# Rebuilding the prologue of a fused Fourier-mixing and gated-FFN kernel

## The chip, the cores and the metric

The kernel runs on one core of a Trainium2 chip. The time is device time in microseconds (us), the median of several executions; lower is better. A core has five engines that work side by side: TensorE (PE in the profile) multiplies matrices, VectorE (DVE) and ScalarE (ACT) work on elements, GpSimd (POOL) does what is left, and SyncE (SP) only issues transfers. They meet at semaphores. Matrix products land in PSUM and the other operands lie in SBUF.

A ratio is the mean time of one kernel's runs over the mean of the other kernel's runs of the same rounds, so it is not quite the ratio of the medians that stand beside it. The profile's span is about 1.8 us shorter than the device time of the same execution.

## The reference

```python
X = np.fft.fft(x, axis=1)                    # x: 8 x 3008 x 256, float32
X = np.fft.fft(X, axis=2)
h = X.real.astype(np.float32).reshape(8 * 3008, 256)
gate = np.maximum(h @ w_gate, 0.0)           # w_gate, w_val: 256 x 1536
val = h @ w_val
out = (gate * val) @ w_out                   # w_out: 1536 x 256
```

The kernel never forms the Fourier transform along the last axis. It folds that transform into the two weight matrices, which it does once, and it exploits symmetry: a real input gives mirrored outputs, so half of the rows are enough for both products.

## The kernel before

Each of the eight batches passes through stage 1 (an add and subtract "fold" of x, then products with a cosine and sine matrix), a shuffle through DRAM, and stage 2. Then come 36 steps of 128 hidden columns: a gate product G, a value product V, their activation gs and product h, and the mirrored pair. The output product po of a step runs 12 steps later. Batch b+1 is prepared inside the steps of batch b. In the steps, GpSimd forms some mirrored products h and, between them, folds the x of a batch two ahead (`fold(b + 2, ...)`). For this text the important part is what runs before the first step, and the weight folds that spill into the first steps.

```python
FIRST = (0, 24, 8, 16)
def fold_first(r):                    # batch 0, 8 rows of 32 at a time, all on VectorE
    ...
    part(lo, 8, 1, ALU.add, False)
    ...                               # subtracts of the same rows
    nc.vector.tensor_copy(...)        # two columns of each row that have no partner

def fold_w(n, i, cs):                 # a weight tile of 512 columns times a 256-row cosine matrix
    ps = pso.tile([128, 512], F32, tag="o", name="psw")
    for c in range(2):                # two fp32 products that accumulate
        nc.tensor.matmul(ps[:], lhsT=cd[c][:, cs, :], rhs=wst[i, n, c][:], start=(c == 0), stop=(c == 1))
    ...                               # copies to wc, ws and (scaled) wm
...
for r in FIRST:
    fold_first(r)
for c0, c1 in ((1, 4), (4, 6), (6, 8), (0, 1)):
    for c in range(c0, c1):
        stage1(0, c, "act")
    shuffle_out(0, c0, c1)
for blk in range(NBLK):
    shuffle_in(0, 4 * blk, 4 * blk + 4)
load_w(1)
load_w(2)
...
nc.gpsimd.tensor_copy(si[0:1, 0:1], wst[1, 2, 1][0:1, 0:1])   # waits for the last weight
load_x(1, nc.sync)                    # a plain load, and a gather that GpSimd issues
for _ in fold(1, nc.gpsimd):
    pass
for i in range(2):
    for cs in range(2):
        fold_w(0, i, cs)              # 4 folds before the first step
rotate(0)
stage2(0, 0, 0, "act")
stage2(0, 0, 1, "dve")
...
for k in range(4):
    at(k, fold_w, 1, k // 2, k % 2)       # 8 folds inside steps 0 to 7
    at(4 + k, fold_w, 2, k // 2, k % 2)
    at(8 + k, stage2, 0, 1 + k // 2, k % 2, "dve")
```

Of the kernel before, what the change touches and what calls it, by code (L numbers as in the profile page):

```python
# [18 lines left out]
RND = 12582912.0  # L19

# [22 lines left out]
def kernel(ctx: ExitStack, tc, x, w_gate, w_val, w_out, out):  # L43
# [67 lines left out]
    FIRST = (0, 24, 8, 16)  # L111

    def load_first():
        xl = xp.tile([96, J, D], F32, tag="xl", name="xl")
        xh = xp.tile([96, NB // 2, D], F32, tag="xh", name="xh")
        for r in FIRST:
            nc.sync.dma_start(out=(xl if r < 16 else xh)[:, r % 16:r % 16 + 8, :],
                              in_=view(x, r * D, [[NB * D, 96], [1, 8 * D]]))
        xt[0] = [xl, xh] + [tp.tile([NA, J, D], BF16, tag="eo", name="eo") for i in range(2)]

    def fold_first(r):
        t, e = xt[0][r // 16][0:NA], xt[0][2 + r // 16]
        lo = r % 16

        def part(a, n, o, op, swap):
            p0 = free(t, a * D + 1, [D, n], [1, H - 1])
            p1 = free(t, a * D + D - 1, [D, n], [-1, H - 1])
            nc.vector.tensor_tensor(e[:, a:a + n, o:o + H - 1], p1 if swap else p0, p0 if swap else p1, op=op)

        part(lo, 8, 1, ALU.add, False)  # L130
        if r == 16:
            part(0, 1, H + 1, ALU.subtract, False)
            part(1, 7, H + 1, ALU.subtract, True)
        else:
            part(lo, 8, H + 1, ALU.subtract, r > 16)
        nc.vector.tensor_copy(free(e[:], lo * D, [D, 8], [H, 2]), free(t, lo * D, [D, 8], [H, 2]))
# [9 lines left out]
    def stage1(b, c, evac):  # L146
# [19 lines left out]
        dst = t1[:, 2 * c:2 * c + 2, :]  # L166
        src = ps[0:96, :].rearrange("p (i d) -> p i d", i=2)
# [47 lines left out]
    nc.gpsimd.iota(ix[:], pattern=[[2 * NA, B]], base=2 * NA - 1, channel_multiplier=-2)  # L215
    nc.gpsimd.tensor_scalar(ix[:], ix[:], scalar1=0, scalar2=None, op0=ALU.max)
    load_first()

# [11 lines left out]
    qpi = const.tile([128, 1], F32, tag="qpi")  # L230


    wst = {}
    for n in range(DF // 512):
        for i in range(2):
            for c in range(2):
                wst[i, n, c] = hp.tile([128, 512], F32, tag="h", name="wst")
    cd = [hp.tile([128, 2, H], F32, tag="h", name="cd") for c in range(2)]

    def load_w(n):  # L240
        for i, w in enumerate((w_gate, w_val)):
# [3 lines left out]
    def fold_w(n, i, cs):  # L245

        ps = pso.tile([128, 512], F32, tag="o", name="psw")
        for c in range(2):
            nc.tensor.matmul(ps[:], lhsT=cd[c][:, cs, :], rhs=wst[i, n, c][:], start=(c == 0), stop=(c == 1))  # L249
        sl_ = slice(n * 512, (n + 1) * 512)  # L250
        if cs == 0:
            nc.scalar.copy(wc[i][:, sl_], ps[:])
        else:
            (nc.scalar.copy if n == 0 else nc.vector.tensor_copy)(ws[i][:, sl_], ps[:])  # L254
            nc.scalar.activation(wm[i][:, sl_], ps[:], ACTF.Copy, scale=s2[:])
# [9 lines left out]
    load_w(0)  # L265

    with tc.tile_pool(name="sp", bufs=1, space=SB) as sp:
        def residue(t, q, n):

            nc.vector.tensor_scalar(q, t, scalar1=1.0 / n, scalar2=RND, op0=ALU.mult, op1=ALU.add)  # L270
            nc.vector.tensor_scalar(q, q, scalar1=-RND, scalar2=float(n), op0=ALU.add, op1=ALU.mult)
            nc.vector.tensor_tensor(t, t, q, op=ALU.subtract)
# [4 lines left out]
        def cosines(out, a, n):  # L277

            nc.scalar.activation(out, a, ACTF.Sin, scale=-2.0 * math.pi / n, bias=qpi[0:a.shape[0], :])


        w1h = sp.tile([NA, 16, 96], BF16, tag="w1h")
        si = sp.tile([NA, NB], F32, tag="si")
        nc.gpsimd.iota(si[:], pattern=[[1, NB]], base=0, channel_multiplier=NB,
                       allow_small_or_imprecise_dtypes=True)
        ki = sp.tile([NA, NKA, 4], F32, tag="ki")
        nc.gpsimd.iota(ki[:], pattern=[[1, NKA], [NKA, 4]], base=0, channel_multiplier=0,
                       allow_small_or_imprecise_dtypes=True)
        nc.vector.memset(qpi[:], math.pi / 2)
        tt = sp.tile([NA, NB, 48], F32, tag="tt")  # L290
        tq = sp.tile([NA, NB, 48], F32, tag="tq")
        nc.vector.tensor_tensor(tt[:], si[:].unsqueeze(2).to_broadcast([NA, NB, 48]),
                                free(ki[:], 0, [0, NB], [1, 48]), op=ALU.mult)
        residue(tt[:], tq[:], S)
        nc.scalar.activation(tq[:], tt[:], ACTF.Abs)
        nc.gpsimd.memset(wz[:], 0.0)
        nc.gpsimd.memset(w1[:, 0, :], 0.0)
# [6 lines left out]

        for r in FIRST:
            fold_first(r)
        for c0, c1 in ((1, 4), (4, 6), (6, 8), (0, 1)):
            for c in range(c0, c1):
                stage1(0, c, "act")
            shuffle_out(0, c0, c1)  # L310
        for blk in range(NBLK):
            shuffle_in(0, 4 * blk, 4 * blk + 4)
        load_w(1)
        load_w(2)


        mi = sp.tile([128, 2], F32, tag="mi")
        nc.gpsimd.iota(mi[:], pattern=[[128, 2]], base=0, channel_multiplier=1,
                       allow_small_or_imprecise_dtypes=True)
        dd = sp.tile([128, 2, H + 1], F32, tag="dd")  # L320
        nc.gpsimd.iota(dd[:], pattern=[[0, 2], [1, H + 1]], base=0, channel_multiplier=0,
                       allow_small_or_imprecise_dtypes=True)
        dq = sp.tile([128, 2, H + 1], F32, tag="dq")
        nc.vector.tensor_tensor(dd[:], dd[:], mi[:].unsqueeze(2).to_broadcast([128, 2, H + 1]), op=ALU.mult)
        residue(dd[:], dq[:], D)
        nc.scalar.activation(dq[:], dd[:], ACTF.Abs)
        for c in range(2):
            cosines(cd[c][:, 0, :], dq[:, c, 0:H], D)
            sines(cd[c][:, 1, 1:H], dd[:, c, 1:H], D, 1.0)
            cosines(cd[c][:, 1, 0:1], dq[:, c, H:H + 1], D)  # L330

        pl = nc.gpsimd


        pi = sp.tile([128, 1], I32, tag="pi")
        nc.gpsimd.iota(pi[:], pattern=[[0, 1]], base=0, channel_multiplier=1)

        def bits(shift, mask):
            ti = sp.tile([128, 1], I32, tag=f"b{shift}{mask}i")
            nc.vector.tensor_scalar(ti[:], pi[:], scalar1=shift, scalar2=mask,  # L340
                                    op0=ALU.logical_shift_right, op1=ALU.bitwise_and)
            tf = sp.tile([128, 1], F32, tag=f"b{shift}{mask}f")
            nc.vector.tensor_copy(tf[:], ti[:])
# [3 lines left out]
        z = sp.tile([128, 1], F32, tag="z")  # L347
        pl.tensor_scalar(z[:], jj[:], scalar1=0.0, scalar2=None, op0=ALU.is_equal)
        zs = sp.tile([128, 1], F32, tag="zs")
        pl.tensor_tensor(zs[:], z[:], sl[:], op=ALU.mult)  # L350
        mul = sp.tile([128, 1], F32, tag="mul")
        pl.tensor_scalar(mul[:], zs[:], scalar1=16.0, scalar2=None, op0=ALU.mult)
        pl.tensor_tensor(mul[:], mul[:], jj[:], op=ALU.add)
        offs = []

        for cs, (o0, d1) in enumerate(((8.0, -8.0), (16.0, -8.0))):
            o = sp.tile([128, 1], F32, tag=f"off{cs}")
            pl.tensor_scalar(o[:], sl[:], scalar1=d1, scalar2=o0 - 8.0, op0=ALU.mult, op1=ALU.add)
            nz = sp.tile([128, 1], F32, tag=f"nz{cs}")
            pl.tensor_scalar(nz[:], z[:], scalar1=-1.0, scalar2=1.0, op0=ALU.mult, op1=ALU.add)  # L360
            pl.tensor_tensor(o[:], o[:], nz[:], op=ALU.mult)
            pl.tensor_scalar(o[:], o[:], scalar1=8.0, scalar2=None, op0=ALU.add)
            offs.append(o)
        kbi = sp.tile([128, 4, NB], F32, tag="kbi")
        nc.gpsimd.iota(kbi[:], pattern=[[0, 4], [1, NB]], base=0, channel_multiplier=0,
                       allow_small_or_imprecise_dtypes=True)
        ui = sp.tile([128, 4, NB], F32, tag="ui")
        nc.gpsimd.iota(ui[:], pattern=[[1, 4], [0, NB]], base=0, channel_multiplier=0,
                       allow_small_or_imprecise_dtypes=True)
        nc.vector.tensor_scalar(ui[:], ui[:], scalar1=up[:], scalar2=None, op0=ALU.is_equal)  # L370
        for cs in range(2):
            t2 = sp.tile([128, 4, NB], F32, tag=f"m2t{cs}")
            nc.vector.tensor_scalar(t2[:], kbi[:], scalar1=mul[:], scalar2=offs[cs][:],
                                    op0=ALU.mult, op1=ALU.add)
            sv = sp.tile([128, 4, NB], F32, tag=f"m2s{cs}")
            sin_of(nc, nc.vector, sp, sv[:], t2[:], NB, [128, 4, NB])
            nc.vector.tensor_tensor(m2[:, cs, :].rearrange("p (u k) -> p u k", u=4), sv[:], ui[:], op=ALU.mult)


        di = sp.tile([128, 4, 2, 16], F32, tag="di")  # L380
        nc.gpsimd.iota(di[:], pattern=[[-32, 4], [-16, 2], [-1, 16]], base=0, channel_multiplier=1,
                       allow_small_or_imprecise_dtypes=True)
        ro = sp.tile([128, 4, 2, 16], F32, tag="ro")
        pl.memset(ro[:], 0.0)
        nc.vector.tensor_scalar(ro[:, :, 0, 1:16], di[:, :, 0, 1:16], scalar1=16.0, scalar2=-1.0,
                                op0=ALU.is_equal, op1=ALU.mult)
# [224 lines left out]
```

## Time and profile before

| what | before |
|---|---|
| device time | 670.34 us median of the first 3 runs (668.94 to 670.45) |
| span of the profiled execution | 667.6 us |
| TensorE busy | 631.9 us (95%) |
| first gate product G starts | 35.23 us |
| first output product po starts | 69.55 us |
| from there to the end | 598.03 us |

These lines are from the profile page: the busy time of each engine (with its share of the span and its number of instructions), and the chain of work that ended last, by engine.

```profile
PE 631.9 (95%) x4157; PEld 413.5 (62%) x4234; DVE 544.4 (82%) x863; ACT 429.2 (64%) x811; POOL 444.9 (67%) x618
...
PE 78%; POOL 9%; issue 5%; DVE 4%; DMA 2%; ACT 1%; SPq 0%; POOLq 0%; DVEq 0%
```

TensorE is the bound engine and only the first 70 us hold much idle time.

Next, the timeline. Columns are start, duration, engine, line of the kernel, operation, output and input with their shapes, and how many records the row joins; the bracket gives the engine's idle time just before and what ended it.

```profile
36.09 1.88 PE L249 MATMUL psw<-wst,cd 128*128 128x512 f32 x4
...
38.14 0.17 POOL L397 COPY si<-wst 1x1 f32<-1x1 f32 x1 [13.18 <-DMA wst<-in_moe_w_val_dram]
38.35 0.60 ACT L437 ACTIVATE gs<-G 128x512 f32<-128x512 f32 x1 [3.17 <-POOL si L397]
...
39.00 0.36 PE L447 MATMUL G<-pq,wm 128*128 128x480 bf16 x1 [1.02 <-ACT gs L437]
...
43.34 1.88 PE L249 MATMUL psw<-wst,cd 128*128 128x512 f32 x4
...
45.05 0.37 PE L447 MATMUL G<-pq,wm 128*128 128x480 bf16 x1
```

A weight fold is four fp32 passes. The next product starts 1.71 us after it (45.05 - 43.34; 1.72 us after others), so eight of them cost about 13.7 us of TensorE inside the steps. The first gs waits 3.17 us for a GpSimd copy that itself waits for the last weight.

At 60.91 ScalarE makes the scaled copy wm of a fold, for which it has waited on VectorE's plain copy ws; gs comes behind it, and TensorE waits for gs:

```profile
60.91 0.69 ACT L255 ACTIVATE wm<-psw,s 128x512 bf16<-128x512 f32 x1 [2.11 <-DVE ws L254]
...
61.94 0.60 ACT L437 ACTIVATE gs<-G 128x512 f32<-128x512 f32 x1
...
62.59 0.36 PE L447 MATMUL G<-pq,wm 128*128 128x480 bf16 x1 [0.96 <-ACT gs L437]
```

The third view is that of one line: the copies of the two unpaired columns on VectorE, with the shortest, median and longest duration in ns. GpSimd is idle at that time.

```profile
L136 DVE CAST eo<-xl x2: 196/198/200, 9.4 to 15.2; 94x16 bf16<-94x16 f32 x2
L136 DVE CAST eo<-xh x2: 199/200/202, 12.0 to 18.3; 94x16 bf16<-94x16 f32 x2
```

### The profile page before, as it was taken

How to read it: one execution, taken by the hardware profiler on the slowest of the kernel's cores; microseconds unless marked ns; L12 is line 12 of the kernel's file. 1: busy time of each engine (PE TensorE's matmuls, PEld its weight loads, DVE VectorE, ACT ScalarE, POOL GpSimd, SP SyncE). 2: the span in 40 equal slices, each digit the busy share in tenths (PEclk: the TensorE clock that was granted, in tenths of full speed). 3: DMA queues.
4: the chain of work that ended last, by engine and by line, in shares of the span. 5: the costliest groups of instructions: out<-in, count | busy, mean ns of one | idle time of the engine just before them, and what ended most of it. 6: DMA issues, size and time to landing. Idle time of an engine off the chain costs nothing.

```text
span 667.6 us, 12589 instructions
## 1 busy us (share of the span) xinstructions
PE 631.9 (95%) x4157; PEld 413.5 (62%) x4234; DVE 544.4 (82%) x863; ACT 429.2 (64%) x811; POOL 444.9 (67%) x618
## 2 busy tenths in 40 slices
PE   1889999999999999999999999999999999999996
PEld 1444666666566666666666666666666766666665
DVE  8446689889788887988888897888889798899991
ACT  5445676676666766676676766676666766666662
POOL 1218559977995599756996499756996455455451
PEclk9999999999999999999999999999999999999999
DMA  9693473185114922177112931258211241211213
GB/s 230 202 239 50 113 182 104 49 204 187 38 56 106 221 89 66 44 163 217 38 44 66 225 128 39 80 132 200 80 48 42 62 127 40 80 31 39 55 32 93
DMA packets 31845, 70.76 MB, mean 106 GB/s; under 512 B 4410, under 2 KB 21426, under 8 KB 29394
## 3 DMA queue, kind: packets, MB, share of 16 engines
q1 hardware_dynamic: 29444, 58.16, 32.0%
q0 software_dynamic: 2336, 11.80, 8.7%
q8 instruction: 33, 0.54, 0.4%
q14 instruction: 32, 0.26, 0.1%
HBM read 39.77 MB, written 30.96 MB: 106 GB/s over the span
## 4 chain that ended last, share of the span: by engine, by line
PE 78%; POOL 9%; issue 5%; DVE 4%; DMA 2%; ACT 1%; SPq 0%; POOLq 0%; DVEq 0%
PE po L503 33%; PE V L459 9%; PE G L436 9%; PE G L447 8%; PE V L457 7%; PE G L435 7%; POOL h L473 4%; POOL eo L101 3%; DMA xh<-in_x_dram 2%; POOL xl L98 2%; PE psw L249 2%; PE V L485 2%; PE ps L159 2%; DVE E L467 1%; PE ps L201 1%
## 5 line engine op out<-in xcount | busy, mean ns | idle before, releaser
L473 POOL TENSOR_TENSOR h<-gm,E 128x480 bf16<-128x480 f32 (+1 forms) x225 | 276.1, 1227 | 154.3 <-DVE E L481 133.9
L503 PE MATMUL po<-wo,h 128*128 128x256 bf16 x2304 | 333.5, 272 | 1.3
L503 PEld LDWEIGHTS <-h 128*128 128x128 bf16 x2304 | 222.7, 98 | 88.0 <-issue 4.4
L450 ACT ACTIVATE gm<-G 128x480 f32<-128x480 f32 (+1 forms) x288 | 167.4, 581 | 140.2 <-PE G L447 109.9
L461 DVE TENSOR_TENSOR h<-gs,V 128x512 bf16<-128x512 f32 x288 | 193.9, 686 | 35.9 <-PE V L459 22.4
L467 DVE SCALAR_TENSOR_TENSOR E<-nb,af,V 128x480 f32<-128x480 bf16 (+1 forms) x225 | 162.9, 724 | 15.6 <-PE V L457 9.1
L437 ACT ACTIVATE gs<-G 128x512 f32<-128x512 f32 x288 | 171.2, 595 | 3.2 <-POOL si L397 3.2
L481 DVE SCALAR_TENSOR_TENSOR E<-E,V 128x480 f32<-128x480 f32 (+1 forms) x225 | 148.0, 658 | 0.0
L447 PE MATMUL G<-pq,wm 128*128 128x480 bf16 (+1 forms) x288 | 106.6, 370 | 7.5 <-ACT gs L437 7.5
L436 PE MATMUL G<-pq,ws 128*128 128x512 bf16 x283 | 107.2, 379 | 2.3
L459 PE MATMUL V<-pq,ws 128*128 128x512 bf16 x284 | 107.5, 378 | 1.7 <-DVE E L467 0.8
L457 PE MATMUL V<-pq,wc 128*128 128x512 bf16 x263 | 99.7, 379 | 0.0
L435 PE MATMUL G<-pq,wc 128*128 128x512 bf16 x245 | 92.8, 379 | 1.0 <-ACT pq L204 1.0
L506 ACT COPY os<-po 128x512 f32<-128x512 f32 x96 | 56.3, 586 | 57.5 <-PE po L503 57.5
L473 DVE TENSOR_TENSOR h<-gm,V 128x480 bf16<-128x480 f32 (+1 forms) x63 | 41.9, 665 | 41.4 <-ACT gm L450 36.1
L101 POOL TENSOR_TENSOR eo<-xl 94x381 bf16<-94x381 f32 x70 | 69.0, 992 | 0.4
L98 POOL TENSOR_TENSOR xl<-xl,xh 94x765 f32<-94x765 f32 x35 | 63.3, 1807 | 2.7
L459 PEld LDWEIGHTS <-ws 128*128 128x128 bf16 x288 | 28.1, 98 | 34.1 <-DVE ws L254 0.4
L436 PEld LDWEIGHTS <-ws 128*128 128x128 bf16 x288 | 28.1, 98 | 32.5 <-issue 1.1
L169 ACT CAST t<-ps 96x512 bf16<-96x512 f32 x64 | 37.4, 584 | 5.8 <-PE ps L157 4.0
L435 PEld LDWEIGHTS <-wc 128*128 128x128 bf16 x288 | 28.1, 98 | 15.1 <-issue 11.5
L457 PEld LDWEIGHTS <-wc 128*128 128x128 bf16 x288 | 28.1, 98 | 13.1 <-issue 4.8
(100 smaller groups left out, 319.3 us busy)
## 6 DMA issues: line engine op xcount, KB each, us to landing
out_dram<-os SPq DMA_DIRECT2D x176, 128.0 KB
xl<-in_x_dram SPq DMA_DIRECT2D x7, 1360.0 KB
Td<-t SPq DMA_DIRECT2D x7, 768.0 KB
t<-Td SPq DMA_DIRECT2D x7, 768.0 KB
nb<-Nd SPq DMA_DIRECT2D x24, 128.0 KB
xl<-in_x_dram SPq DMA_DIRECT2D x7, 238.0 KB
xl<-in_x_dram SPq DMA_DIRECT2D x2, 768.0 KB
xh<-in_x_dram SPq DMA_DIRECT2D x2, 768.0 KB
```

The source lines that it names most:

```text
L435: nc.tensor.matmul(e["G"][:], lhsT=wc[0][:, fs], rhs=pq[:, 0, :], start=True, stop=False)
L436: nc.tensor.matmul(e["G"][:], lhsT=ws[0][:, fs], rhs=pq[:, 1, :], start=False, stop=True)
L437: nc.scalar.activation(e["gs"][:], e["G"][:], ACTF.Relu)
L447: nc.tensor.matmul(e["G"][:, cols], lhsT=wm[0][:, f * 128:(f + 1) * 128], rhs=pqt[b, blk][:, 1, cols], start=False, stop=True, skip_group_ ...
L450: nc.scalar.activation(e["gm"][:, cols], e["G"][:, cols], ACTF.Relu)
L457: nc.tensor.matmul(e["V"][:], lhsT=wc[1][:, fs], rhs=pq[:, 0, :], start=True, stop=split(t))
L459: nc.tensor.matmul(e["V"][:], lhsT=ws[1][:, fs], rhs=pq[:, 1, :], start=False, stop=True, skip_group_check=split(t))
L461: nc.vector.tensor_tensor(e["h"][:, 0, :], e["gs"][:], e["V"][:], op=ALU.mult)
L467: nc.vector.scalar_tensor_tensor(e["E"][:, cols], nbt[b, blk][:, cols], af[:, f:f + 1], e["V"][:, cols], op0=ALU.mult, op1=ALU.add)
L473: eng.tensor_tensor(free(e["h"][:], 512 + cols.start + NB - 1, [NB, (cols.stop - cols.start) // NB], [-1, NB]), e["gm"][:, cols].rearrange ...
L481: nc.vector.scalar_tensor_tensor(e["E"][:, cols], e["E"][:, cols], 2.0, e["V"][:, cols], op0=ALU.mult, op1=ALU.subtract)
L503: nc.tensor.matmul(po[:, s % 2, :], lhsT=ht[t - f + ff]["h"][:, sg, g * 128:(g + 1) * 128], rhs=wo[:, ff, :], start=(ff == 0), stop=(ff == ...
```

## The change

Five things are meant to shorten the prologue. Batch 0 arrives in pieces of 4 rows, so that less work follows the last piece. Its subtracts go to GpSimd while VectorE does the adds. The rows of the weights are paired (sum and difference), so that a fold needs two products of 64 output columns in place of two of 128; these can lie side by side in the array. TensorE gets 32 products on zeros at the start, to bring its clock up. The weights are loaded in another order and the copy that held gs back goes.

```diff
-    FIRST = (0, 24, 8, 16)
+    FIRST = (0, 28, 4, 24, 8, 20, 12, 16)
...
-    def fold_w(n, i, cs):
-        ps = pso.tile([128, 512], F32, tag="o", name="psw")
-        for c in range(2):
-            nc.tensor.matmul(ps[:], lhsT=cd[c][:, cs, :], rhs=wst[i, n, c][:], start=(c == 0), stop=(c == 1))
+    def pair_w(n, i, eng):
+        lo, hi, up = (wst[i, n, c] for c in range(3))
+        eng.tensor_tensor(up[:], lo[:], hi[:], op=ALU.add)
+        eng.tensor_tensor(lo[:], lo[:], hi[:], op=ALU.subtract)
+    def fold_w(n, i, cs, evac="act"):
+        ps = ...
+        for k, w in ((0, wst[i, n, 2]), (1, wst[i, n, 0])):
+            nc.tensor.matmul(ps[64 * k:64 * k + 64, :], lhsT=cd[:, cs, 64 * k:64 * k + 64], rhs=w[:],
+                             start=True, stop=True)
...
+        dve.memset(wk[:], 0.0)
+        for k in range(WARM):              # WARM = 32
+            nc.tensor.matmul(ps[:], lhsT=wk[:, 512:640], rhs=wk[:, 0:512], start=True, stop=True)
...
-        for r in FIRST:
-            fold_first(r)
+        for r in (0, 24):
+            fold_first(r, 8, ALU.add, dve)
+        for r in FIRST[4:]:
+            fold_first(r, 4, ALU.add, dve)
+        for r in FIRST[:-2]:
+            fold_first(r, 4, ALU.subtract, pl)
+        for r in FIRST[-2:]:
+            fold_first(r, 4, ALU.subtract, dve)
...
+        pair_w(0, 0, dve)
...
+        pair_w(1, 0, pl)
+        pair_w(1, 1, dve)
...
-        nc.gpsimd.tensor_copy(si[0:1, 0:1], wst[1, 2, 1][0:1, 0:1])
+        pl.tensor_copy(seen[:, 0:1], t4t[0][0:1, NKA - 1, 0:1])
         load_x(1, nc.sync)
...
+        for i in range(2):
+            pair_w(2, i, pl)
...
     rotate(0)
-    stage2(0, 0, 0, "act")
+    fold_w(1, 1, 0, "act")
...
+    at(0, fold_w, 1, 1, 1, "dve")
     for k in range(4):
-        at(k, fold_w, 1, k // 2, k % 2)
-        at(4 + k, fold_w, 2, k // 2, k % 2)
+        at(3 + k, fold_w, 2, k // 2, k % 2, "dve" if k % 2 else "act")
...                                        # the plan of batch 1's stage 1 and stage 2 moves by 1 or 2 steps
```

## The prediction

> **What bounds the kernel now.** The page gives TensorE 631.9 of 667.6 us. In the windows view it is over 95% busy from 70 to 650 us, so that part should not move. What can move is the first 60 us, read from the engines' timelines:
> - Batch 0 arrives in four pieces; the last is awaited until 15.93, its VectorE fold ends at 18.46, and five stage-1 chunks follow at one per 0.86 us (TensorE 4 x 0.213 us, half the rate of later matmuls). The last copy ends at 22.92.
> - Weight folds: 16 fp32 passes, 23.73 to 33.33 (9.77 us), the first half at half rate. A warm fold is 1.72 us. They hold the rotation back; first gate product G at 35.23.
> - The first gate activation, gs, then waits until 38.35 for a GpSimd copy that waits for the last weight DMA. 2 to 3 us lost.
> - Eight more folds run inside steps 0 to 7, 1.72 us each: 13.8 us on TensorE, the bound engine.
>
> **What the change does.**
> 1. Folds in the loop: 5 instead of 8, and each is two 64-column products that should run side by side. The Trainium skill, "TensorE: Matmul & The Clock Gate", Part 3, says products in different column groups run concurrently; nothing in this trace shows it for fp32. An fp32 product is two passes of 0.43 us; if only the second pass of one overlaps the first of the next, a lone fold takes three passes, 1.28 us (estimate): 6.4 us instead of 13.8, a gain of 7.4. Fully serial: a gain of 5.2. All of it is critical.
> 2. The wait of gs for the last weight goes (the copy is gone): about 2.7 us.
> 3. Warm-up products: 32, ending near 10 us (estimate from 0.43 then 0.213 us each). Stage 1 cannot start before about 13, so TensorE may be slow again: gain under 1 us.
> 4. Start of the first G. Three chunks instead of five follow the last piece: about 2.5 us earlier. The rate of loading stays (250 GB/s), so the last piece still lands near 16. Twelve pairing passes come on VectorE (about 0.69 us) and GpSimd (about 1.3 us, estimated from 765 elements in 1.80 us). Without interference I get first G near 30.5.
> 5. Against it: the Trainium skill, "SBUF — State Buffer", "Who interferes with whom", says a VectorE instruction with two SBUF inputs and a GpSimd instruction that reads SBUF exclude each other. Six subtracts of 508 elements (1.26 us each, estimate), a product and a residue on GpSimd would then block VectorE's adds. This trace has no such overlap to test it. If it holds, the folds end near 24 instead of 18.4, and the first G is at 36 to 38, later than now.
>
> **Sum.** Without exclusion: 4.7 + 2.7 + 7.4, about 15 us: 655. With it: -2 + 2.7 + 7.4, about 8 us: 662. I give exclusion 60%. Prediction 658.5 us, range 652 to 666; chances: faster by over 2% 0.36, within 2% 0.61, slower 0.03.
>
> **What would show it.** Fold products starting 0 to 0.43 us apart in pairs, 1.28 us a fold; gs following G at once; first G before 33 (no exclusion) or after 35; GpSimd subtracts and VectorE adds taking turns, with durations stretched to over 1.5 us, if exclusion holds; stage-1 chunks at 0.43 us if the warm-up lasts, 0.86 if not; steps after 80 us unchanged.
>
> **What would make it wrong.** Column groups not overlapping for fp32; stage 1's strided PSUM copies being slower in every batch; early weight DMA delaying the shuffle.

## The result, and the profile after

| what | before | after |
|---|---|---|
| device time, median | 669.82 us (668.94 to 670.45, 4 runs) | 661.89 us (661.60 to 662.38, 4 runs) |
| ratio | | 0.9884, 95% interval 0.9870 to 0.9898 |
| span of the profiled execution | 667.6 us | 660.6 us |
| first G starts | 35.23 us | 34.69 us |
| first output product po starts | 69.55 us | 62.71 us |
| from there to the end | 598.03 us | 597.90 us |

The change gains 1.2%. In the profile all of it lies ahead of the first output product: 0.54 us to the first G, then 6.30 us between G and po (34.32 us became 28.02 us).

The page after, same two lines:

```profile
PE 637.0 (96%) x4266; PEld 410.1 (62%) x4266; DVE 553.3 (84%) x871; ACT 426.7 (65%) x809; POOL 468.8 (71%) x630
...
PE 81%; POOL 11%; DVE 5%; issue 2%; ACT 1%; POOLq 0%; DVEq 0%
```

(TensorE shows more busy time than before although it finishes earlier: 32 warm-up products take 9.09 us, and the first profile lacks more matmul records.)

The timeline after, first in batch 0's folds, then in the first steps:

```profile
12.15 0.67 DVE L130 TENSOR_TENSOR eo<-xl 94x508 bf16<-94x508 f32 x1
12.16 1.78 POOL L130 TENSOR_TENSOR eo<-xl 94x508 bf16<-94x508 f32 x1
...
12.75 1.24 DVE L134 CAST eo<-xl 94x8 bf16<-94x8 f32 x1
...
13.89 0.67 DVE L130 TENSOR_TENSOR eo<-xh 94x508 bf16<-94x508 f32 x1
13.91 1.60 POOL L130 TENSOR_TENSOR eo<-xh 94x508 bf16<-94x508 f32 x1
...
36.16 1.08 PE L261 MATMUL psw<-wst,cd 128*64 128x512 f32 x4
...
37.17 0.38 PE L483 MATMUL G<-pq,wm 128*128 128x480 bf16 x1
...
38.01 0.69 ACT L269 ACTIVATE wm<-psw,s 128x512 bf16<-128x512 f32 x1 [1.49 <-DVE ws L268]
...
39.05 0.60 ACT L473 ACTIVATE gs<-G 128x512 f32<-128x512 f32 x1
...
39.70 0.36 PE L483 MATMUL G<-pq,wm 128*128 128x480 bf16 x1 [1.08 <-ACT gs L473]
```

Four things are to be seen. VectorE's copy of 8 elements starts at 12.75 and ends at 13.99, when GpSimd's subtract (12.16 to 13.94) ends; then both engines go on together. The subtract waits in its turn: all six of GpSimd's subtracts end 1.12 us (on xl) or 0.95 us (on xh) after the end of the add that VectorE started beside them, whether that add took 0.67 or 1.20 us. A fold now takes 1.01 us (37.17 - 36.16) in place of 1.71. And the wait behind wm now comes twice, at 39.70 and at 53.98, where the kernel before had it once: wm waits for VectorE's copy ws of the same PSUM tile, gs queues behind it, and TensorE idles 1.08 us for gs.

The view of the copies' line after, against about 200 ns before:

```profile
L134 DVE CAST eo<-xl x3: 1240/1240/1260, 8.9 to 16.1; 94x8 bf16<-94x8 f32 x2, 94x16 bf16<-94x16 f32 x1
L134 DVE CAST eo<-xh x3: 1065/1067/1085, 11.2 to 17.8; 94x8 bf16<-94x8 f32 x2, 94x16 bf16<-94x16 f32 x1
```

And the windows view after (length of the stretch, busy us and count of each engine, then the granted TensorE clock, the DMA share and GB/s):

```profile
10.00:15.00 5.00, 1.71 (x9) 0.84 (x8) 5.00 (x7) 4.39 (x7) 5.00 (x4) 1.00 1.03 277
15.00:20.00 5.00, 3.12 (x14) 2.56 (x14) 5.00 (x8) 1.74 (x3) 4.69 (x8) 0.56 0.82 286
20.00:25.00 5.00, 4.48 (x20) 3.00 (x20) 3.81 (x14) 1.75 (x3) 3.85 (x10) 0.50 0.37 101
```

The clock that the warm-up had bought is gone when most of stage 1 runs: TensorE had work for only 1.71 of the 5 us from 10 to 15, and from 15.5 its products start 0.21 us apart, where they started 0.11 apart at 13.6.

The result can be added up in part from the starts of products. (A product's record lasts 0.38 us though the next can start after 0.21, so a wait costs about 0.17 us more than the bracket shows.)

| term | us gained |
|---|---|
| first G | 0.54 |
| folds in the steps, 8 x 1.72 became 5 x 1.01 | 8.7 |
| the wait of TensorE for the first gs | 1.2 |
| the wait of TensorE for gs behind wm, once before (at 62.59) | 1.1 |
| waits of TensorE after: twice 1.26 for gs behind wm, 0.52 for the second half of pq, 0.41 for h | -3.45 |
| not taken apart (smaller gaps between products) | -1.25 |
| sum: first output product earlier | 6.84 |

The spans differ by 7.0 us.

### The profile page after: what moved, and what is told of

The parts are those of the page before. It is cut to its first block, busy times and chain, and to the rows that moved or that the text cites. A ratio compares the mean times of both kernels' runs of the same rounds, so it can differ in the third digit from the quotient of the medians.

```text
span 660.6 us, 12759 instructions
## 1 busy us (share of the span) xinstructions
PE 637.0 (96%) x4266; PEld 410.1 (62%) x4266; DVE 553.3 (84%) x871; ACT 426.7 (65%) x809; POOL 468.8 (71%) x630
## 4 chain that ended last, share of the span: by engine, by line
PE 81%; POOL 11%; DVE 5%; issue 2%; ACT 1%; POOLq 0%; DVEq 0%
PE po L539 33%; PE V L495 9%; PE V L493 8%; PE G L472 8%; PE G L471 8%; PE G L483 8%; POOL h L509 3%; POOL eo L102 3%; POOL xl L99 2%; PE V L521 2%; PE ps L162 2%; POOL eo L130 2%; DVE E L503 1%; PE psw L261 1%; PE ps L204 1%
## 5 line engine op out<-in xcount | busy, mean ns | idle before, releaser
L495 PE MATMUL V<-pq,ws 128*128 128x512 bf16 x288 | 109.0, 378 | 1.1 <-DVE E L503 0.5
L472 PE MATMUL G<-pq,ws 128*128 128x512 bf16 x288 | 109.1, 379 | 0.4 <-DVE pq L209 0.4
L471 PE MATMUL G<-pq,wc 128*128 128x512 bf16 x288 | 109.1, 379 | 0.0
L493 PE MATMUL V<-pq,wc 128*128 128x512 bf16 x288 | 109.1, 379 | 0.0
```

Of the source, the lines that this page charges most:

```text
L471: nc.tensor.matmul(e["G"][:], lhsT=wc[0][:, fs], rhs=pq[:, 0, :], start=True, stop=False)
L472: nc.tensor.matmul(e["G"][:], lhsT=ws[0][:, fs], rhs=pq[:, 1, :], start=False, stop=True)
L493: nc.tensor.matmul(e["V"][:], lhsT=wc[1][:, fs], rhs=pq[:, 0, :], start=True, stop=split(t))
L495: nc.tensor.matmul(e["V"][:], lhsT=ws[1][:, fs], rhs=pq[:, 1, :], start=False, stop=True, skip_group_check=split(t))
```

## The experiments

Three theories were on the table. A: VectorE and GpSimd exclude each other in batch 0's folds, and that costs the prologue its gain. B: the subtracts on GpSimd are merely slow, or the loads set the pace, and the copies' length is of no account. C, formed later: from a certain point the time is set by another chain, GpSimd's, and no longer by the first output product.

Twelve kernels ran, all correct, in three groups; each group ran on a chip of its own and has its own runs of the kernel before (medians 669.64, 669.68 and 669.04 us, 11 runs each), so kernels of different groups are best compared by their ratios. "First G" and "first po" are starts in the profiled execution.

| run | median us (range, runs) | ratio to before (95%) | first G | first po |
|---|---|---|---|---|
| e1_folds_dve | 660.15 (658.80 to 661.74, 5) | 0.9857 (0.9835 to 0.9879) | 32.07 | 60.09 |
| e2_full_folds | 665.81 (665.22 to 666.33, 6) | 0.9944 (0.9926 to 0.9961) | 35.79 | 66.94 |
| e3_no_warm | 664.54 (663.21 to 665.16, 6) | 0.9924 (0.9906 to 0.9941) | 34.69 | 62.72 |
| e4_before_release | 668.97 (667.06 to 671.04, 6) | 0.9985 (0.9962 to 1.0007) | 34.77 | 67.81 |
| c_after_again | 661.27 (660.38 to 663.56, 4) | 0.9871 (0.9856 to 0.9886) | 36.18 | 64.20 |
| e5_no_warm_again | 664.07 (661.46 to 665.61, 6) | 0.9916 (0.9897 to 0.9935) | 34.70 | 62.72 |
| e6_prologue | 662.20 (660.32 to 665.15, 6) | 0.9888 (0.9865 to 0.9911) | 31.83 | 64.96 |
| e7_prologue_steps | 660.26 (658.91 to 662.46, 5) | 0.9858 (0.9839 to 0.9878) | 31.82 | 63.85 |
| e8_pair_early | 659.08 (657.66 to 660.62, 5) | 0.9841 (0.9820 to 0.9862) | 32.14 | 58.23 |
| e9_late_load | 657.87 (656.81 to 658.95, 5) | 0.9826 (0.9807 to 0.9845) | 32.24 | 58.34 |
| e10_pair_first | 659.21 (658.97 to 660.42, 5) | 0.9851 (0.9832 to 0.9869) | 31.14 | 57.24 |
| e11_wm_late | 661.86 (659.75 to 663.38, 6) | 0.9885 (0.9863 to 0.9907) | 34.68 | 60.69 |

### Taking GpSimd out of batch 0's folds (e1_folds_dve)

```diff
-        for r in (0, 24):
-            fold_first(r, 8, ALU.add, dve)
-        for r in FIRST[4:]:
+        for r in FIRST:
             fold_first(r, 4, ALU.add, dve)
-        for r in FIRST[:-2]:
-            fold_first(r, 4, ALU.subtract, pl)
-        for r in FIRST[-2:]:
             fold_first(r, 4, ALU.subtract, dve)
```

> The changed kernel with one thing altered: all batch 0 subtracts run on VectorE, piece by piece (add, copy, subtract), none on GpSimd. Theory A (VectorE and GpSimd exclude each other on two-input work, so the second engine bought nothing): the 16-element copies fall from about 1.1 us back to 0.2 us, the folds end at 18 to 19 us instead of 20.1, the last stage-1 copy at or before 22 instead of 23.3, first G at 31 to 33.5 instead of 34.7, and the kernel is 1 to 4 us faster than the changed kernel (658 to 661 us). Theory B (the engines do overlap and GpSimd is merely slow): VectorE gets 6 x 0.6 us more work, folds end near 24 us, first G later, kernel 2 to 4 us slower (664 to 666 us).

The copies' line in this run:

```profile
L134 DVE CAST eo<-xl x4: 171/172/174, 8.4 to 16.0; 94x8 bf16<-94x8 f32 x4
L134 DVE CAST eo<-xh x4: 170/172/174, 9.6 to 17.3; 94x8 bf16<-94x8 f32 x4
```

One engine alone is faster than the two together: the folds end at 18.1 us in place of 20.1, the copies are back at 0.17 us, and the first G comes 2.62 us earlier, as does the first po. That is what theory A says. The total, however, gains only about half of it (660.15 against 661.3 to 661.9): the next batch takes 78.80 us from its first po to the following one, where the changed kernel takes 77.32. That loss is taken up under theory C.

### Undoing the pairing of the weights (e2_full_folds)

```diff
-        for k, w in ((0, wst[i, n, 2]), (1, wst[i, n, 0])):
-            nc.tensor.matmul(ps[64 * k:64 * k + 64, :], lhsT=cd[:, cs, 64 * k:64 * k + 64], rhs=w[:],
-                             start=True, stop=True)
+        for k, (cw, w) in enumerate(((cd, wst[i, n, 0]), (cd1, wst[i, n, 1]))):
+            nc.tensor.matmul(ps[:], lhsT=cw[:, cs, :], rhs=w[:], start=(k == 0), stop=(k == 1))
```

(`pair_w` does nothing in this run, and `cd1` is the second cosine matrix.)

> The changed kernel with the pairing of weight rows undone: each fold is again two full-width fp32 products that accumulate, no pairing passes; everything else as in the changed kernel. Theory A (half-width products side by side are what gained): a fold takes 1.72 us again instead of about 1.1 us, five of them in the loop cost about 3 us, and the seven ahead of the first G hold TensorE until about 36, so first G at 37 to 38.5; kernel 4 to 7 us slower than the changed one (666 to 669 us). Theory B (twelve pairing passes on VectorE and GpSimd cost in the prologue what the products save): first G no later than 34.7, total within 2 us of the changed kernel.

The timeline of TensorE in this run:

```profile
22.29 11.39 PE L260 MATMUL psw<-wst,cd 128*128 128x512 f32 x24
33.52 0.39 PE L204 MATMUL ps<-m,t 128*128 128x128 bf16 x4
```

The time rises by about 4 us, at the edge of what was expected, and the first po by 4.23 us. The first G moved less than expected (35.79 us). Pairing is thus worth about 4 us in the changed kernel, of the 7.9 us that the whole change gains.

### Leaving out the warm-up products (e3_no_warm, e5_no_warm_again)

```diff
-WARM = 32
+WARM = 0
```

> The changed kernel without its 32 warm-up products. Theory A (TensorE is slow again from about 15.5 us on whatever was done before 10 us): stage-1 chunks after 16 us stay at 0.86 us each, first G within 0.5 us of 34.7, total within 1 us of the changed kernel. Theory B (the warm-up keeps the clock up where it matters): more than 1.5 us slower.

> The kernel without warm-up products once more, now beside the changed kernel. The two profiles agree to 0.02 us at the first gate product and at the first output product, so theory A (the warm-up buys nothing) expects a total within 1 us of the control; theory B (it costs something later that the profile of one run did not show) expects 2 us or more slower again.

The profiles of both runs agree with the changed kernel's up to the first po within 0.01 us (62.72 against 62.71). Yet both are slower than it in the timed runs: 664.54 and 664.07 us, against 661.89 and, in the same rounds as the second, 661.27. So about 2.7 us hang on the warm-up, in two groups, and the prediction's "under 1 us" is wrong. No view shows how. In the second run's profile the load of x for batch 1 landed 0.7 us later than in the changed kernel's and the second batch's first po came 0.9 us later; in the first run's profile neither is so. The profiled executions help little here: that of e3 is the fastest of its six runs, that of the changed kernel the slowest of its four, and their spans differ by only 0.8 us. e3's theory B got its number, but its reason, a higher clock where it matters, is not seen. The cause stays open.

### Releasing gs in the kernel before (e4_before_release)

```diff
-        nc.gpsimd.tensor_copy(si[0:1, 0:1], wst[1, 2, 1][0:1, 0:1])
+        nc.gpsimd.tensor_copy(seen[:], wst[1, 2, 1][0:1, 0:1])
```

> The kernel before with one thing altered: the one-element GpSimd copy that waits for the last weight DMA writes to a constant tile, so that the pool of temporary tiles is free before and gs need not wait. As predicted, 2.7 us would go. As the trace is read now, TensorE did a fold in that wait and only 1.0 us of it was idle, so the gain is 0.7 to 1.3 us (668.5 to 669.2 us beside 669.8).

The copy that waits for the last weight wrote into `si`, a tile of the prologue's pool whose memory gs takes over. With a tile of its own as the target, gs need not wait for it. The timeline of ScalarE:

```profile
35.46 0.60 ACT L438 ACTIVATE gs<-G 128x512 f32<-128x512 f32 x1 [0.74 <-PE G L437]
```

The wait is gone, and the first po comes 1.74 us earlier, of which 0.46 us is an earlier first G; the other 1.28 us agree with the 1.2 us read above. In the total nothing can be told (0.9985, interval 0.9962 to 1.0007). The prediction's 2.7 us was too much.

### The changed kernel once more (c_after_again)

> Control: the changed kernel itself, on the same chip and beside the same runs of the kernel before as the other kernels of this group. Expected ratio 0.988 to the kernel before, as in its first measurement, so 661 to 663 us; if it comes out at 0.990 or above, the slower total of the kernel without warm-up in the last group was the chip and not the warm-up.

It repeats at 661.27 us. Its profiled execution shows how TensorE's clock varies: the 16 passes of four weight folds took 5.77 us in place of 4.38, because the clock was still low, and the first G came at 36.18. So one profile's first G is good to about 1.5 us.

### Building a better prologue (e6_prologue, e7_prologue_steps)

In e6_prologue VectorE alone folds batch 0, as in e1, and computes the small tables; the fourth weight tile is loaded ahead of the shuffle; and fill-in products on zeros stand between the stage-1 chunks, to hold the clock. A sixth weight fold moves into the steps. Cut to its core, against the changed kernel:

```diff
-        for c0, c1, ev in ((1, 4, "aaa"), (4, 6, "aa"), (6, 8, "ad"), (0, 1, "a")):
+        load_w(1, (1,))
+        for c0, c1, fill in ((1, 4, (5, 0, 6)), (4, 6, (0, 8)), (6, 8, (0, 0)), (0, 1, (0,))):
             for c in range(c0, c1):
-                stage1(0, c, "act" if ev[c - c0] == "a" else "dve")
+                stage1(0, c, "act")
+                filler(fill[c - c0])
...
-        load_w(1, (1,))
...
-        pair_w(1, 0, pl)
-        pair_w(1, 1, dve)
+        pair_w(1, 0, dve)
...
     rotate(0)
-    fold_w(1, 1, 0, "act")
+    pair_w(1, 1, nc.vector)
     stage2(0, 0, 1, "dve")
```

> The changed kernel with its prologue arranged for what the runs showed: nothing on GpSimd that reads while VectorE works on two inputs (products, residue, folds, small columns and the pairing for the first two thirds all on VectorE), fillers that keep TensorE busy between stage-1 chunks, the last weights of the second third loaded ahead of the shuffle, pairing passes ahead of the second-stage tables. If exclusion and TensorE's slow clock are what held the prologue: folds end at 17 to 18 us, stage-1 chunks at about 0.5 us, first G at 28 to 31 us (34.7 in the changed kernel). The total gains less, since loads of batch 1 start only 2 to 4 us earlier: 657 to 660 us. If something else holds it: first G above 33.

e7_prologue_steps adds that the scaled copy wm is issued a step later (which meets the wait of gs behind wm), and that two stage-2 copies go to ScalarE:

```diff
-    at(1, fold_w, 1, 1, 1, "act")
+    at(1, fold_w, 1, 1, 1, "dve", 2)        # 2: the step in which wm is issued
...
-        at(3 + k, fold_w, 2, k // 2, k % 2, "dve" if k % 2 else "act")
-        at(8 + k, stage2, 0, 1 + k // 2, k % 2, "dve")
+        at(3 + k, fold_w, 2, k // 2, k % 2, "dve" if k % 2 else "act", 4 + k)
+        at(8 + k, stage2, 0, 1 + k // 2, k % 2, "act" if k % 2 else "dve")
```

> As the one before, and in the first steps the scaled copy of a fold waits one step, so that it does not stand ahead of the next gate activation on ScalarE behind VectorE's copy of the same bank, and two of the four second-stage copies of steps 8 to 11 go to ScalarE. The two waits of 1.08 us of TensorE for gs in the first steps should go and the steps 8 to 11 shorten by up to 0.3 us each: 2 to 3 us less at the first output product than the one before, total 1 to 3 us less.

e6 missed its first G and its total. e7 met its total (1.9 us less than e6) and missed its first po, which came 1.1 us earlier than e6's and not 2 to 3. The clock held: stage-1 products start 0.11 us apart, a chunk takes 0.44 us in place of 0.86, and the last stage-1 copy ends at 19.7 us where the changed kernel's ends at 23.27. But the first G came only at 31.8, and the second product of that step 3.0 us (e6) and 3.7 us (e7) after it. The timeline of e7 shows why:

```profile
30.24 1.13 POOL L442 DMA_DIRECT2D wo<-in_moe_w_out_dram  x1
...
30.57 2.65 DVE L253 TENSOR_TENSOR wst<-wst 128x512 f32<-128x512 f32 x1
...
31.37 1.29 POOL L253 TENSOR_TENSOR wst<-wst 128x512 f32<-128x512 f32 x1
...
32.75 1.60 POOL L254 TENSOR_TENSOR wst<-wst 128x512 f32<-128x512 f32 x1
33.26 1.63 DVE L254 TENSOR_TENSOR wst<-wst 128x512 f32<-128x512 f32 x1
34.31 1.71 POOL L253 TENSOR_TENSOR wst<-wst 128x512 f32<-128x512 f32 x1
34.82 0.68 DVE L209 CAST pq<-ps 128x512 bf16<-128x512 f32 x1
...
35.55 0.58 PE L478 MATMUL G<-pq,ws 128*128 128x512 bf16 x1 [3.35 <-DVE pq L209]
```

The pairing of the fourth weight tile on VectorE met GpSimd's own pairing. From 31.37 the two took turns, and the copy pq that TensorE needed stood behind it. The rebuilt prologue had walked into the same exclusion in another place.

Pairing is not the whole of it. When VectorE's add started at 30.57, GpSimd was still issuing the load of wo, until 31.37. In e6 the same add lay beside two such issues alone:

```profile
29.98 1.16 POOL L85 DMA_INDIRECT xh<-in_x_dram,ix  x1 [0.88 <-DMA wst<-in_moe_w_val_dram]
30.58 1.73 DVE L253 TENSOR_TENSOR wst<-wst 128x512 f32<-128x512 f32 x1
31.15 1.13 POOL L441 DMA_DIRECT2D wo<-in_moe_w_out_dram  x1
32.29 1.29 POOL L253 TENSOR_TENSOR wst<-wst 128x512 f32<-128x512 f32 x1
```

It took 1.73 us and ended when the second issue did. In the changed kernel, however, two such operations beside the issue of the gather took 0.68 and 0.69 us (at 31.49 and 32.20). What held VectorE up during the issues stays open. TensorE's idle time also cost it its clock: the next weight fold of e7 took 1.98 us.

### Moving that pairing into idle time (e8_pair_early)

```diff
         pair_w(1, 0, dve)
+        pair_w(1, 1, dve)
...
     rotate(0)
-    pair_w(1, 1, nc.vector)
     stage2(0, 0, 1, "dve")
```

> The rebuilt prologue of e7_prologue_steps with one edit: the sum and difference of the fourth weight tile (value weights, columns 512 to 1023) on VectorE move ahead of the Nyquist rotation, into the 2.4 us in which VectorE sat idle (28.04 to 30.49 us), before GpSimd starts its own pairing. Theory A (in e7 the two operations were long only because GpSimd's pairing ran beside them): they fall from 2.65 and 1.63 us to about 0.7 each, the second G moves from 35.5 to about 32, the first output product from 63.85 to about 60.5, total about 657. Rival B (they were long for another reason, such as operands that had only just landed, or the gain comes back later): durations or the first output product stay within 1 us of e7, total 660 or more.

The timeline of e8:

```profile
28.33 0.68 DVE L253 TENSOR_TENSOR wst<-wst 128x512 f32<-128x512 f32 x1
29.05 0.69 DVE L254 TENSOR_TENSOR wst<-wst 128x512 f32<-128x512 f32 x1
...
31.19 1.29 POOL L253 TENSOR_TENSOR wst<-wst 128x512 f32<-128x512 f32 x1
...
31.50 0.69 DVE L209 CAST pq<-ps 128x512 bf16<-128x512 f32 x1 [0.49 <-PE ps L204]
```

The same two instructions on the same operands, out of GpSimd's way, take 0.68 and 0.69 us in place of 2.65 and 1.63, and the copy pq comes 3.3 us earlier. The move took them out of the way of the load of wo as well, so e8 does not separate its issue from the pairing. For batch 0's folds, e1 and the taking of turns settle theory A. The first po comes at 58.23, 5.62 us earlier than in e7 and 4.48 earlier than in the changed kernel. But the total is 659.08, 2 us above what was expected. Most of the gain is given back after the first po.

### Where it is given back (e9_late_load, e10_pair_first, e11_wm_late)

Three runs of the same rounds as e8 say where.

e9_late_load, against e8, moves one load:

```diff
-        load_w(1, (1,))
         for c0, c1, fill in ((1, 4, (5, 0, 6)), (4, 6, (0, 8)), (6, 8, (0, 0)), (0, 1, (0,))):
             ...
             shuffle_out(0, c0, c1)
+        load_w(1, (1,))
```

> As e8_pair_early, and the load of the fourth weight tile is issued behind the writes of the shuffle instead of ahead of them. Theory A (the load, ahead in the queue, held the shuffle back): the first read-back of the shuffle is issued about 1 us earlier than in e7 (22.93 us), the shuffled tile is seen before 28.0 us, first G about 31, total about 656. Rival B (the shuffle is bound by the last stage-1 copy at 19.7 us and by its own latency): the read-back starts within 0.3 us of e7's.

e10_pair_first, against e9, moves one pairing ahead of the stage-2 matrix:

```diff
         pair_w(0, 1, dve)
+        pair_w(1, 0, dve)
         fold_w(0, 0, 0)
...
-        pair_w(1, 0, dve)
         pair_w(1, 1, dve)
```

> As e9_late_load, and VectorE pairs the third weight tile before it computes the stage-2 matrix, so that its two folds (1.07 us each) run on TensorE while it waits for the shuffle, not between the shuffle's end and the first stage-2 product. Expected: stage-2 products start when the shuffled tile lands (within 0.3 us), 1 to 2 us earlier than in e8, first G about 30, first output product about 59, total about 655. Rival: the stage-2 matrix, now 1.4 us later, or the copies of the four folds, hold the first G at e9's time, and the total is the same within 1 us.

e11_wm_late is the changed kernel with the late scaled copy alone:

```diff
-            nc.scalar.activation(wm[i][:, sl_], ps[:], ACTF.Copy, scale=s2[:])
+            rest = lambda: nc.scalar.activation(wm[i][:, sl_], ps[:], ACTF.Copy, scale=s2[:])
+            rest() if late is None else at(late, rest)
...
-    at(0, fold_w, 1, 1, 1, "dve")
+    at(0, fold_w, 1, 1, 1, "dve", 1)
...
-        at(3 + k, fold_w, 2, k // 2, k % 2, "dve" if k % 2 else "act")
+        at(3 + k, fold_w, 2, k // 2, k % 2, "dve" if k % 2 else "act", 4 + k)
```

> The changed kernel with one edit: ScalarE's scaled copy of a folded tile, which waited for VectorE's plain copy out of the same PSUM bank three times, is issued one step later. Theory: the two waits of TensorE for gs of 1.08 us in the first batch go, first G unchanged at about 34.7, G to first output product 28.0 falls to about 26, total about 659.3 (2 us less than the changed kernel's 661.3 to 661.9). Rival: ScalarE's wait was not on the chain (VectorE's own chain from h to V sets the step), and the stretch stays above 27.5.

e11 did to the first po just what was expected: 28.02 us between G and po became 26.01, and both waits of 1.08 us are gone. Its total did not move (661.86 us). e10 has the earliest first po of all, 57.24 us, yet its total is 659.21 (655 expected), 1.3 us slower than e9, whose first po comes 1.1 us later. So beyond some point an earlier first po is worth nothing. The chain of waits of e8 (start, duration, what) shows what is worth something. In the stretch from 28 to 95 us it does not run through TensorE at all:

```profile
28.82 19.62 DMA xh<-in_x_dram,ix
...
48.57 0.23 POOL eo L97
...
73.02 17.40 DMA xl<-in_x_dram
...
90.84 1.80 POOL xl L99
```

A gather of x for batch 1 lands, GpSimd folds batch 1, the load of batch 2 can start because its buffers are free, it lands, and GpSimd folds batch 2, between its mirrored products h. When that last fold is late against TensorE's steps, the products h are late too, and TensorE waits for them by way of VectorE. The timeline of e8:

```profile
107.99 0.71 DVE L509 SCALAR_TENSOR_TENSOR E<-nb,af,V 128x480 f32<-128x480 bf16 x1 [1.37 <-POOL h L515]
...
108.75 0.38 PE L501 MATMUL V<-pq,ws 128*128 128x512 bf16 x1 [0.99 <-DVE E L509]
```

e11 shows the same thing later, in the windows view from 120 to 130 us. First the changed kernel, where TensorE is busy 9.96 of 10 us:

```profile
120.00:130.00 10.00, 9.96 (x74) 6.84 (x73) 8.09 (x14) 7.59 (x15) 9.92 (x15) 1.00 0.21 51
```

Then e11, where it is busy 8.79 and GpSimd (the fifth figure) all of the time:

```profile
120.00:130.00 10.00, 8.79 (x63) 5.86 (x61) 7.11 (x12) 6.30 (x13) 10.00 (x16) 1.00 0.18 60
```

Starts read from the timelines turn this into a rule, a fit to one profiled execution of each kernel. "Fold 1" and "fold 2" are GpSimd's first instruction on the x of batch 1 and 2; "po 1" is the first output product of the second batch.

| run | first po | fold 1 | fold 2 | po 1 | po 1 - fold 2 | po 1 - first po |
|---|---|---|---|---|---|---|
| before | 69.55 | 51.96 | 97.00 | 146.54 | 49.54 | 76.99 |
| e2_full_folds | 66.94 | 49.51 | 93.99 | 143.83 | 49.84 | 76.89 |
| e7_prologue_steps | 63.85 | 46.40 | 90.90 | 140.79 | 49.89 | 76.94 |
| after | 62.71 | 50.07 | 91.72 | 140.03 | 48.31 | 77.32 |
| e5_no_warm_again | 62.72 | 50.77 | 92.64 | 140.95 | 48.31 | 78.23 |
| e11_wm_late | 60.69 | 49.69 | 91.29 | 139.57 | 48.28 | 78.88 |
| e1_folds_dve | 60.09 | 48.96 | 90.59 | 138.89 | 48.30 | 78.80 |
| e8_pair_early | 58.23 | 48.57 | 90.55 | 138.82 | 48.27 | 80.59 |
| e9_late_load | 58.34 | 45.56 | 87.23 | 135.55 | 48.32 | 77.21 |
| e10_pair_first | 57.24 | 46.94 | 90.06 | 138.36 | 48.30 | 81.12 |

The second batch starts either 76.9 us after the first, which is taken as TensorE's own pace (76.89 to 76.99 where fold 2 leaves room), or 48.3 us after GpSimd's fold 2 began, whichever is later. In seven of these ten runs it is the second, to within 0.03 us. (The four profiles not in the table fit as well: there po 1 comes 48.33 to 48.81 us after fold 2, and no first batch is shorter than 76.90. The next batch takes 77.2 to 78.6 us in these profiles; what sets it was not looked at.) The kernel before had 1.2 us to spare there. The changed kernel already stands at the limit. e1, e8, e10 and e11 moved the first po by 2 to 5.5 us and GpSimd's chain by less, and lost the difference. e9 moved both: its x for batch 1 landed 4.5 us earlier than in the changed kernel, and with it fold 2, and its whole gain in first po of 4.4 us arrives at po 1 (135.55 against 140.03). In the total 3.4 to 4.0 us of it remain (657.87 against 661.27 and 661.89).

Why x landed 3 us earlier in e9 than in e8 is not settled: the gather was issued only 0.4 us earlier and took 17.0 us in place of 19.6, beside the same other loads in another order. Part of this may be chance: between two executions of one kernel the gather's time differed by 1.5 us (18.7 and 20.2 in the changed kernel's two profiles) and by 1.2 us (18.2 and 19.4 without warm-up). e9's own expectations were met for the shuffle (read-back issued at 21.74 in place of 22.93) and missed for the total (656) and for the first G (32.24, not 31), because two weight folds still stood ahead of stage 2. e10 brought the first G to 31.14 (30 expected) and shows that it was worth nothing. Loading the x of batch 1 earlier was not run; by the rule it is the next thing to try.

e9_late_load beats both kernels: 657.87 us, 0.9826 of the kernel before (interval 0.9807 to 0.9845). Its lead over e8 (0.9841, 0.9820 to 0.9862) is not clear of the noise.

## Why the prediction was right or wrong

The prediction said 658.5 us with a range of 652 to 666, and gave 0.61 to a change within 2%. Measured were 661.89 us and a ratio of 0.9884. The range and the class hold. The 658.5 was a mean of two branches, 655 without exclusion and 662 with it, and the branch with exclusion came true almost to the tenth. That closeness is partly luck, since its terms were wrong in both directions.

- **Exclusion of VectorE and GpSimd: right, given 60%.** The Trainium skill, "SBUF — State Buffer", section "Who interferes with whom", says that whoever comes first of two such instructions holds the shared pair of ports for the whole instruction; on VectorE's side it names two-input instructions with both inputs in SBUF (against a GpSimd instruction that reads SBUF), and copies and casts that can use both ports. A cast of 8 elements went from 0.17 us to 1.24 us (e1 against the changed kernel), and a two-input add from 0.68 to 2.65 us (e8 against e7), 1.3 us of it beside a pairing pass of GpSimd. The same section says that VectorE instructions with one SBUF input at most, outside those two-port copies, do not contend; here h (inputs gs in SBUF and V in PSUM) took 0.69 us at 36.55 beside GpSimd's pairing (36.24 to 37.51), and 0.68 us at 44.75 in the kernel before, with GpSimd idle.
- **"The folds end near 24 instead of 18.4, and the first G is at 36 to 38": mis-sized.** They ended at 20.1 and the first G came at 34.69 (36.18 in the other profile of the same kernel). The engines took turns, but the turns were short: a subtract needed 0.95 to 1.12 us once the add beside it was over, against the 1.26 of the prediction's estimate (with that wait its record lasts 1.60 to 2.17), VectorE's adds ran at their full pace of 0.67, and of VectorE's work only the small copies waited for a subtract.
- **"Three passes, 1.28 us": mis-sized.** A lone fold took 1.01 us. In the trace the products start in pairs, at 36.157 and 36.164, then at 36.637 and 36.644: full overlap, where the estimate allowed for half. The Trainium skill, "TensorE: Matmul & The Clock Gate", Part 3, puts some 4 ns between the starts of products that are packed into the array; here it is 7 ns, for fp32 in two column groups. The gain in folds was 8.7 us, not 7.4. With the pairing undone (e2) the time rises by about 4 us.
- **"The wait of gs goes: about 2.7 us": mis-sized.** The bracket of 3.17 us stands at ScalarE, which is not the bound engine. TensorE had a weight fold to do meanwhile and lost 1.2 us. In e4 the release alone moved the first po by 1.74 us.
- **"Gain under 1 us" for the warm-up: wrong in the timed runs, right in the profiles.** Without it two groups of runs are about 2.7 us slower. The step that failed is the argument that only stage 1 could profit; what profits instead is open. The part about the clock was right: TensorE was slow again from 15.5 us. The skill's Part 1 of the same page puts the return to half rate after an idle window of about 3.4 us; here it came although no idle gap after the warm-up was over 1.52 us, with TensorE at work for 1.71 of 5 us.
- **Missing from the sum: waits in the steps.** With the faster fold, TensorE waits twice 1.26 us for gs behind wm behind ws, where the kernel before waited once, 1.1 us, and 0.93 us for pq and h: 2.3 us more in all. e11 takes the two away and brings the first po 2.02 us forward. The prediction's own worry, stage-1 copies slower in every batch, did not come: ScalarE took 585 ns for one, and 584 before.
- **"Steps after 80 us unchanged": right, and only just.** The changed kernel's second batch takes 77.32 us where TensorE alone would take 76.9. The profile before hinted at the reason, 9% of the chain on GpSimd (11% after), and the prediction did not ask what that chain would do once the first batch came earlier. e8 and e11 show what more gain before the first po would have met: of 2.02 us in e11, 0.46 reached po 1.

## What to carry to other kernels

Before a prologue is shortened, look for every chain that leads from it into the steady state, and not only for the bound engine's: here a gather, a fold on GpSimd and a second load set the start of the second batch, and once the kernel stood at that limit, gains ahead of the first output product counted only when that chain moved as well. Do not split work over VectorE and GpSimd when both read SBUF with instructions that need the shared ports; one engine alone was faster, and the same exclusion waits at any other place where the two meet. A wait at an engine that is not the bound one is worth only what the bound engine lacks meanwhile, so read it from that engine's gap.

## What the Trainium skill lacked or had wrong

- "TensorE: Matmul & The Clock Gate", Part 3, gives its measured speedups for blocks of 32 and none for fp32 or blocks of 64 columns. Here two 64-column fp32 products of 512 columns ran in step, 7 ns apart, and a lone fold of two took 1.01 us where two full-width ones took 1.71: 1.7 times as fast, not 2 times. In a row of four folds (from 30.2 us on) a pair of passes started every 0.43 us, 0.86 us a fold, which is twice as fast.
- The same page, Part 1, tells of the return to half rate after an idle window. It speaks of frequent short gaps too, but puts no number to them: here the clock fell between 15.5 and 16 us after a stretch with 1.71 us of work in 5 and no idle gap over 1.52 us, and in another execution of the same kernel a later stretch stayed slow: 16 passes took 5.77 us in place of 4.38.
- The same page warns that a trace's clock events are unreliable and tells of a clock seen stuck low, but not of half rate that goes unseen. Here the granted clock in the windows view missed half rate: the kernel before shows 1.00 from 15 to 25 us while its stage-1 products start 0.21 us apart, against 0.11 in e6 and e7.
- "SBUF — State Buffer", "Who interferes with whom", agrees with every instruction pair that was tested here. It has a measured slowdown of 6.8 times for VectorE without the shape behind it; here a cast of 8 elements took 1.24 us in place of 0.17, seven times as long, since it waits for the rest of a GpSimd instruction of 1.8 us. It tells of VectorE holding up the issue of GpSimd's DMAs and not of the reverse: in e6 a two-input add took 1.73 us in place of 0.68 while GpSimd did nothing but issue DMAs (cause open).
- No page that was consulted gives the time of a gather that GpSimd issues among other loads: here that of batch 1 took 12.8 to 20.2 us from issue to landing over the fourteen profiles, and up to 1.5 us more or less in two executions of one kernel.
